# Attention scores: the whole-array block in front of the row pairs, and a later mix

## The chip, the cores and the metric

The kernel runs on one core of a Trainium2 chip. The metric is the device time of one execution in microseconds (us); the median of several runs is compared.

## What is computed

The inputs have batch 4, 12 heads, 448 positions and 64 channels a head. The first part is an attention with a sigmoid in place of the softmax; its result goes through a gated network whose input is mixed with the position before, and this through a network with a Fourier transform ahead of it:

```python
def _attn_ref(q, k, v):
    S = q.shape[2]
    scores = np.matmul(q, k.transpose(0, 1, 3, 2)) / np.sqrt(q.shape[-1]) - np.log(S)
    return np.matmul(1.0 / (1.0 + np.exp(-scores)), v)

def _moe_ref(x, mu_k, mu_r, w_k, w_v, w_r):
    x_prev = ...                      # x, one position earlier
    xk = mu_k * x + (1.0 - mu_k) * x_prev
    xr = mu_r * x + (1.0 - mu_r) * x_prev
    k = np.maximum(xk @ w_k, 0.0)
    v = k * k @ w_v
    return v / (1.0 + np.exp(-(xr @ w_r)))

def _moe2_ref(x, w_ch1, w_ch2):
    u = x + np.real(np.fft.fft(np.fft.fft(x, axis=1), axis=2))
    un = (u - mean(u)) / np.sqrt(var(u) + 1e-06)
    return u + np.maximum(un @ w_ch1, 0.0) @ w_ch2
```

The change lies in the attention and in the first mix (xk).

## The kernel before

Two heads of one batch make a pair; there are 24 pairs, six a batch. For a pair the scores are made transposed, keys on the partitions, in seven blocks of up to 128 x 448 (`places`): three row pairs, in which the two heads use the upper and the lower 64 rows of the TensorE array at the same time (blocks 0 and 1, 2 and 3, 4 and 5), and one block that uses the whole array for the last keys of both heads (`FULL`, block 6). Each block goes to ScalarE (ACT), which takes the sigmoid into a tile `sg` (`weigh`). The blocks of the row pairs are in PSUM banks of a pool of five (`ps2`), in rotation, so the sixth block of a pair takes the bank of its first; the whole-array block is in a pool of three (`ps1`), which the value product and the keys use too.

The first six pairs (`WHOLE`) use 32-bit matmuls. From pair 6 on, q and k are split in a high and a low part, and each block is three matmuls (high by high, low by high, high by low). There `scores` issues the whole-array block first in pairs 6 and 7 and last in pairs 8 to 23.

`attnv` then multiplies the seven sigmoid tiles with v: the value product, tile `av`. `join` copies it to x on ACT, stores x to memory for a later stage, and mixes it with the position before (`mix`: ACT scales, VectorE adds, ACT and VectorE split the result in a high and a low part `xkh` and `xkl`). When a batch has its six mixes, `keys` multiplies them with `w_k`: 8 tiles of 18 matmuls a batch, tile `k`.

The order of every engine's instructions is written by a planner at build time (`Order`). It keeps a clock `now` that TensorE's instructions advance by charged costs; every task is a generator that yields the time at which it goes on. `others()` lets tasks that are due issue their work, but no key matmul. `issued(key)` waits until the planner has noted that key; it adds no instruction and no semaphore. Key matmuls wait in a queue (`feed`) and are issued one by one when nothing else is due. The loop is `attention`: pass i issues the value product of pair i - 1, then the scores of pair i, and then holds the next pass until `PACE` = 10.8 planner microseconds have gone since its start, if there is key work (`pace`). What the planner charges is not what the chip takes.

At the same time `prepare` loads and splits q, k and v of later pairs, and `weights` loads and converts weights on VectorE at a pace of its own (`EVERY`). Behind the attention the rest of the keys runs, and then the other stages, to which nothing is changed.

Of the kernel before, what the change touches and what calls it, by code (L numbers as in the profile page):

```python
# [27 lines left out]
GF = 256  # L28
NG = FF2 // GF
TOK = B * S  # L30
PACE = 10.8
EVERY = (11.6, 9.4)

SL = np.r_[np.arange(2, 129, 2), np.arange(1, 128, 2)]
# [210 lines left out]
def build(tc, ap):  # L245
    nc = tc.nc
    V, G = nc.vector, nc.gpsimd
    o = Order(nc)
# [81 lines left out]
    def bank(name):  # L330
        return ps1.tile([128, 512], F32, tag="bank", name=name)
# [16 lines left out]
    pairs = [(b, p) for b in range(B) for p in range(NP)]  # L348
    WHOLE = NP
# [26 lines left out]
    FULL = len(places) - 1  # L376

    def weigh(i, n, ps):
        sg = att.tile([128, S], F32, tag="sg", name=f"sg_{i}_{n}", bufs=len(places) + 1)
        o.at["sg", i, n] = o.act(sg, ps[:, 0:S], AF.Sigmoid, bias=bias_s, scale=1.0 / math.sqrt(DH))  # L380
        sg_t[i, n] = sg

    def scores(i):
        k, q = pair_t["k", i], pair_t["q", i]

        def rows(j):
            return slice(0, 128) if j is None else slice(64 * j, 64 * j + 64)

        def room(n):
            name = f"sc_{i}_{n}"  # L390
            return bank(name) if n == FULL else ps2.tile([128, 512], F32, tag="sc", name=name)

        if i < WHOLE:
            for n in [FULL, *range(FULL)]:
                c, j = places[n]
                ps = room(n)
                o.mm(ps[:, 0:S], k[rows(j), c], q[rows(j)], True, True, 0.760 if j is None else 0.447)
                weigh(i, n, ps)
                yield from o.others()
        else:  # L400
            halves = [(2 * c, 2 * c + 1) for c in range(3)]
            for ns in [(FULL,), *halves] if i < WHOLE + 2 else [*halves, (FULL,)]:
                ps = {n: room(n) for n in ns}
                for t, (a, b) in enumerate(((0, 0), (0, 1), (1, 0))):
                    for n in ns:
                        c, j = places[n]
                        cost = None if j is None else 0.107
                        o.mm(ps[n][:, 0:S], k[a][rows(j), c], q[b][rows(j)], t == 0, t == 2, cost)
                for n in ns:
                    weigh(i, n, ps[n])  # L410
                yield from o.others()
        o.at["pair", i] = o.now

    def attnv(i, ps):
        v = pair_t["v", i]
        for n in [FULL, *range(FULL)]:
            yield from o.need(("sg", i, n))
            c, j = places[n]
            sg = sg_t.pop((i, n))
            if j is None:  # L420
                o.mm(ps[:, 0:S], v[:, c].rearrange("p j d -> p (j d)"), sg, True, False, 0.760, skip=True)
            else:
                me = slice(64 * j, 64 * j + 64)
                o.mm(ps[me, 0:S], v[:, c, j], sg, False, c == 2, 0.432, skip=True)
            yield from o.others()
        o.at["av", i] = o.now
        o.spawn(join(i, ps), o.now + 0.2)

    def join(i, ps):
        x = att.tile([128, S + 1], F32, tag="x", name=f"x_{i}")  # L430
        G.memset(x[:, 0:1], 0.0)
        yield o.act(x[:, 1 : S + 1], ps[:, 0:S])
        b, p = pairs[i]
        o.dma(x_d[b][p], x)
        if b > 1:
            yield from o.issued(("key", b - 2))
        xh = mop.tile([128, S], F32R, tag=f"xkh{p}", name=f"xkh_{i}")
        xl = mop.tile([128, S], F32R, tag=f"xkl{p}", name=f"xkl_{i}")
        xk_t[b, p] = (xh, xl)
        yield from mix(x, mu_k, att, p, f"k{i}", xh, xl, ("xk", b, p))  # L440
        o.at["mixed", i] = o.now

    def mix(x, mu, pl, p, nm, xh, xl, key, bufs=2):
        xk = pl.tile([128, S], F32, tag="mix", name=f"mix_{nm}", bufs=bufs)
        yield o.act(xk, x[:, 1 : S + 1], AF.Copy, scale=mu[:, 0, p : p + 1])
        yield o.stt(xk, x[:, 0:S], mu[:, 1, p : p + 1], xk, ALU.mult, ALU.add)
        yield o.act(xh, xk)
        o.at[key] = t = o.sub(V, xl, xk, xh)
        yield t
# [6 lines left out]
    def attention():  # L456
        for i in range(len(pairs) + 1):
            t0 = o.now
            if i > 0:
                yield from o.need(("v", i - 1), ("sg", i - 1, FULL))  # L460
                if i > 2:
                    yield from o.issued(("mixed", i - 3))
                yield from attnv(i - 1, bank(f"av_{i - 1}"))
            if i < len(pairs):
                yield from o.need(("k", i), ("q", i))
                yield from scores(i)
            yield t0 + pace()
        yield from o.need(("xk", B - 1, NP - 1))
        o.at["attention"] = o.now

    def pace():
        return PACE if o.feed else 0.0

# [872 lines left out]
```

## Time and profile before

| | us |
|---|---|
| median of 3 runs | 1226.49 |
| lowest, highest | 1226.11, 1231.38 |
| the profiled execution | 1231.31 |
| its span, first to last instruction | 1229.5 |
| granted TensorE clock over the span | 1.000 (the 2.4 GHz level) |

In the trace PE is the matmuls of TensorE, PEld its weight loads, DVE VectorE, ACT ScalarE, POOL GpSimd, SP the engine that issues the DMAs. Rows have times from the span's start; a row of the timeline gives start, duration, engine, line, operation, and what it writes and reads (out<-in). A matmul's duration covers its pipeline, so the rows of matmuls that follow each other overlap; the step from start to start is what one costs. The tiles are named sc (scores), sg (sigmoid), av (value product), x (its copy), mix_k (the mix) and k (keys).

### The profile page before, as it was taken

Reading aid. Unit: us, or ns where it says so; the run is one execution under the profiler, and the core shown is the slowest. Engines: PE = TensorE matmul, PEld = TensorE weight load, DVE = VectorE, ACT = ScalarE, POOL = GpSimd, SP = SyncE. Lnnn points to the kernel's source line nnn. Section 1 sums busy time; section 2 is a strip of 40 time slices with the busy share of each in tenths; the row PEclk is TensorE's granted clock in tenths of the full one; section 3 lists DMA queues with packets and bytes.
Section 4 is the critical chain, followed back from the end, with each engine's and each line's share of the span. In section 5 each row is a group of like instructions: output and inputs, shape, how many; then the busy total and the mean of one; then the engine's idle time right before and its main releaser. Section 6 shows DMA issues by size and latency. Waiting matters only on the chain. (4 is left out here: it accounts for less than half of the span.)

```text
span 1229.5 us, 16416 instructions
## 1 busy us (share of the span) xinstructions
PE 1216.5 (99%) x6142; PEld 1050.5 (85%) x6142; DVE 907.4 (74%) x1425; ACT 479.1 (39%) x864; POOL 135.3 (11%) x97
## 2 busy tenths in 40 slices
PE   8999999999999999999989999999999999999998
PEld 3467766789999998999979999999999999999998
DVE  5776887656853669797999999897566776776654
ACT  5867767766530122142333333332132332322220
POOL 0000000000000000000232232222021111121110
PEclk9999999999999999999999999999999999999999
DMA  6656669666948446396555555555842112121102
GB/s 219 223 169 229 213 239 339 237 243 231 320 158 259 169 165 218 113 316 227 184 202 212 184 200 203 201 186 188 314 141 78 52 54 75 52 66 63 52 1 90
DMA packets 77296, 217.82 MB, mean 177 GB/s; under 512 B 9312, under 2 KB 31776, under 8 KB 76576
## 3 DMA queue, kind: packets, MB, share of 16 engines
q1 hardware_dynamic: 76544, 214.37, 50.3%
q0 software_dynamic: 672, 2.40, 0.6%
q8 instruction: 48, 0.79, 0.3%
q14 instruction: 32, 0.26, 0.1%
HBM read 143.84 MB, written 72.90 MB: 176 GB/s over the span
## 5 line engine op out<-in xcount | busy, mean ns | idle before, releaser
L215 DVE TENSOR_TENSOR acc<-acc,f 128x448 f32<-128x448 f32 x258 | 156.6, 616 | 66.4 <-PE f L180 63.8
L180 PE MATMUL f<-h,w2h 128*128 128x448 f32 x576 | 165.6, 368 | 3.6 <-DVE acc L215 3.6
L180 PE MATMUL f<-un,w1h 128*128 128x448 f32 x576 | 166.2, 368 | 0.0
L180 PE MATMUL f<-h,v2h 128*128 128x448 f32 x576 | 163.6, 365 | 0.0
L180 PEld LDWEIGHTS f<-h,w2h 128*128 128x128 f32 x576 | 107.8, 188 | 14.9 <-DVE acc L215 4.8
L234 ACT ACTIVATE sg<-sc,bias_s 128x448 f32<-128x448 f32 x168 | 95.0, 651 | 60.7 <-PE sc L180 60.7
L180 PEld LDWEIGHTS f<-un,w1h 128*128 128x128 f32 x576 | 108.2, 188 | 10.4 <-issue 0.4
L180 PEld LDWEIGHTS f<-h,v2h 128*128 128x128 f32 x576 | 108.2, 188 | 8.5
L180 PE MATMUL v<-k,wvh 128*128 128x448 f32 x384 | 113.4, 370 | 0.8 <-DMA k<-k_d 0.7
L180 PE MATMUL f<-un,w1l 128*128 128x448 f32 x288 | 105.9, 368 | 0.0
L180 PE MATMUL f<-h,w2l 128*128 128x448 f32 x288 | 105.9, 368 | 0.0
L180 PE MATMUL f<-h,v2l 128*128 128x448 f32 x288 | 105.2, 365 | 0.0
L223 DVE SCALAR_TENSOR_TENSOR w_bits<-w_raw,w_bits 128x768 uint32<-128x768 uint32 x80 | 99.9, 1248 | 1.0
L180 PE MATMUL av<-sg,v 128*64 128x448 f32 (+1 forms) x336 | 81.1, 549 | 0.0
L180 PEld LDWEIGHTS v<-k,wvh 128*128 128x128 f32 x384 | 71.6, 188 | 8.1 <-DMA k<-k_d 2.4
L215 POOL TENSOR_TENSOR v2l<-v,v2h 128x768 fp32r<-128x768 f32 x24 | 46.8, 1970 | 275.0 <-ACT v2h L232 275.0
L215 POOL TENSOR_TENSOR w1l<-w,w1h 128x768 fp32r<-128x768 f32 x20 | 41.2, 2062 | 300.6 <-ACT w1h L232 295.5
L180 PE MATMUL v<-k,wvl 128*128 128x448 f32 x192 | 70.8, 369 | 0.0
L180 PE MATMUL k<-xkh,wkh 128*128 128x448 f32 x192 | 70.7, 368 | 0.0
L180 PE MATMUL k<-xkl,wkh 128*128 128x448 f32 x192 | 70.4, 367 | 0.0
L180 PE MATMUL k<-xkh,wkl 128*128 128x448 f32 x192 | 70.3, 366 | 0.0
L180 PEld LDWEIGHTS av<-sg,v 128*64 128x64 f32 (+1 forms) x336 | 27.9, 144 | 42.5 <-issue 35.9
(175 smaller groups left out, 2356.7 us busy)
## 6 DMA issues: line engine op xcount, KB each, us to landing
w_raw<-in_w SPq DMA_DIRECT2D x40, 768.0 KB, 4.5
w_d<-w SPq DMA_DIRECT2D x40, 384.0 KB, 2.6
k_d<-kp SPq DMA_DIRECT2D x32, 448.0 KB, 2.8
k<-k_d SPq DMA_DIRECT2D x32, 448.0 KB, 6.3
a<-w_d SPq DMA_DIRECT2D x24, 384.0 KB, 3.5
v<-w_d SPq DMA_DIRECT2D x24, 384.0 KB, 3.0
k<-in_k SPq DMA_DIRECT2D x24, 256.0 KB, 5.5
v<-in_v SPq DMA_DIRECT2D x24, 256.0 KB, 3.0
```

Source lines behind the costliest of these rows:

```text
L180: self.nc.tensor.matmul(out, lhs, rhs, start=start, stop=stop, skip_group_check=skip)
L215: eng.tensor_tensor(out, a, c, op=op)
L223: self.nc.vector.scalar_tensor_tensor(out, a, scalar, c, op0=op0, op1=op1)
L234: self.nc.scalar.activation(out, a, fn, **kw)
```

## The change

`PACE` falls from 10.8 to 10.6. From pair 8 on the whole-array block is issued first too. In `join`, behind the copy and the store of x, the mix of pair i is held back until the planner has issued the scores of pair i + 1; the last pair's mix is not held.

```diff
--- before.py
+++ after.py
@@ -28,7 +28,7 @@
 GF = 256
 NG = FF2 // GF
 TOK = B * S
-PACE = 10.8
+PACE = 10.6
 EVERY = (11.6, 9.4)
 
 SL = np.r_[np.arange(2, 129, 2), np.arange(1, 128, 2)]
@@ -399,7 +399,7 @@
                 yield from o.others()
         else:
             halves = [(2 * c, 2 * c + 1) for c in range(3)]
-            for ns in [(FULL,), *halves] if i < WHOLE + 2 else [*halves, (FULL,)]:
+            for ns in [(FULL,), *halves]:
                 ps = {n: room(n) for n in ns}
                 for t, (a, b) in enumerate(((0, 0), (0, 1), (1, 0))):
                     for n in ns:
@@ -432,6 +432,8 @@
         yield o.act(x[:, 1 : S + 1], ps[:, 0:S])
         b, p = pairs[i]
         o.dma(x_d[b][p], x)
+        if i + 1 < len(pairs):
+            yield from o.issued(("pair", i + 1))
         if b > 1:
             yield from o.issued(("key", b - 2))
         xh = mop.tile([128, S], F32R, tag=f"xkh{p}", name=f"xkh_{i}")
```

## Rows read from the trace of the kernel before

**Rows 1.** The page: busy time, share of the span and instructions of each engine.

```profile
PE 1216.5 (99%) x6142; PEld 1050.5 (85%) x6142; DVE 907.4 (74%) x1425; ACT 479.1 (39%) x864; POOL 135.3 (11%) x97
```

**Rows 2.** Waits of PE's matmuls: engine, line, releaser; us in total, times, longest.

```profile
PE f L180 <- DVE acc L215: 3.6, 2, 2.0
```

**Rows 3.** Windows, one pass (pair 8): us; busy us (instructions) by engine; clock, DMA.

```profile
66.56:78.09 11.53, 11.53 (x63) 8.05 (x61) 8.56 (x14) 9.17 (x18) 0.10 (x1) 1.00 0.59 187
```

**Rows 4.** Waits of the weight loads (PEld) from 62 to 250 us: total, times, longest.

```profile
PEld sc L180 <- ACT sg L234: 4.6, 16, 0.3
```

**Rows 5.** Timeline, pair 10, row pairs first: start us, us, engine, line, operation, out<-in.

```profile
89.64 0.48 PE L180 MATMUL sc<-qh,kh 64*128 64x448 f32 x2
...
90.55 1.16 ACT L234 ACTIVATE sg<-sc,bias_s 128x448 f32<-128x448 f32 x2 [2.29 <-PE sc L180]
...
91.60 0.53 ACT L232 COPY x<-av 128x448 f32<-128x448 f32 x1
92.01 2.75 ACT L234 ACTIVATE sg<-sc,bias_s 128x448 f32<-128x448 f32 x5
...
92.04 0.47 PE L180 MATMUL sc<-qh,kh 128*128 128x448 f32 x1
...
92.75 0.36 PE L180 MATMUL k<-xkl,wkh 128*128 128x448 f32 x1
...
92.96 0.36 PE L180 MATMUL k<-xkh,wkl 128*128 128x448 f32 x1
...
94.60 0.72 ACT L234 ACTIVATE mix_k<-x,mu_k 128x448 f32<-128x448 f32 x1
...
97.82 3.32 PE L180 MATMUL av<-sg,v 128*128 128x448 f32 x14
```

**Rows 6.** Timeline, pair 6, whole-array block first; the last row is pass 7's value product.

```profile
49.11 0.47 PE L180 MATMUL sc<-qh,kh 128*128 128x448 f32 x1
...
49.63 0.36 PE L180 MATMUL sc<-qh,kl 128*128 128x448 f32 x1
...
49.92 0.47 PE L180 MATMUL sc<-qh,kh 64*128 64x448 f32 x2
...
50.02 0.64 ACT L234 ACTIVATE sg<-sc,bias_s 128x448 f32<-128x448 f32 x1 [1.41 <-PE sc L180]
...
50.56 0.53 ACT L232 COPY x<-av 128x448 f32<-128x448 f32 x1
...
50.97 2.22 ACT L234 ACTIVATE sg<-sc,bias_s 128x448 f32<-128x448 f32 x4
...
52.48 3.85 PE L180 MATMUL av<-sg,v 128*128 128x448 f32 x14
```

**Rows 7.** Timeline, pair 7, whole-array block first, and the first key matmuls behind it.

```profile
56.26 0.47 PE L180 MATMUL sc<-qh,kh 128*128 128x448 f32 x1
...
56.41 0.54 ACT L232 COPY x<-av 128x448 f32<-128x448 f32 x1 [0.18 <-issue]
...
57.73 0.66 ACT L234 ACTIVATE mix_k<-x,mu_k 128x448 f32<-128x448 f32 x1
...
58.29 1.15 ACT L234 ACTIVATE sg<-sc,bias_s 128x448 f32<-128x448 f32 x2
...
59.76 0.47 PE L180 MATMUL k<-xkh,wkh 128*128 128x448 f32 x1
...
60.07 0.36 PE L180 MATMUL k<-xkl,wkh 128*128 128x448 f32 x1
```

**Rows 8.** Timeline, the value products of passes 4 and 6.

```profile
31.00 3.42 PE L180 MATMUL av<-sg,v 128*128 128x448 f32 x14
...
45.52 3.66 PE L180 MATMUL av<-sg,v 128*128 128x448 f32 x14
```

**Rows 9.** Timeline, pass 23: the value product and the first scores.

```profile
234.95 3.32 PE L180 MATMUL av<-sg,v 128*128 128x448 f32 x14
...
243.56 0.47 PE L180 MATMUL sc<-qh,kh 64*128 64x448 f32 x2
```

## The prediction

> **What bounds the kernel now.** I read the page first, then who TensorE waits for, then one pass of the attention loop row by row. TensorE is busy for 99% of the span, the other engines for much less [rows 1], and over the whole program the waits of its matmuls are small: two waits on VectorE far behind the stage of the change come to 3.6 us [rows 2]. In the stage of the change one pass of the loop takes 11.53 us, of which PE is busy 11.53 us, DVE 8.56 and ACT 9.17 [rows 3]; this row is typical of the passes of pairs 8 to 21. So the stage ends when TensorE's program is through: keys, scores and values share one in-order queue, there is always key work in it, and a stall of TensorE is paid in full. What does not delay TensorE here is free.
>
> "Busy 100%" does not mean that there is no stall, since a matmul row covers its pipeline too. The weight-load rows show it: in the sixteen passes with split scores behind pair 7, a score weight load stood idle for a sigmoid 16 times, 4.6 us in all, 0.3 us at most [rows 4]. Therefore I count from start to start, not busy time.
>
> **The old pass (pair 10) [rows 5].** Scores start at 89.64, the whole-array block at 92.04, the first key matmul at 92.75: 3.11 us. The first sigmoid starts 0.91 us after the first score matmul. The sixth row block needs the bank of the first (five banks), so it waits for that sigmoid; from the start of the sigmoid of block 0 to the end of the third row pair it is 92.04 - 90.55 = 1.49 us. The key matmuls then run from 92.75 to 97.82, 25 of them at 0.20 us; from the first to the second it is 0.21 us.
>
> **Whole-array block first.** Pairs 6 and 7 already run in the new order, so the trace before holds the experiment. In pair 6 [rows 6] ACT takes the sigmoid of the whole-array block at +0.91 us (50.02 - 49.11), then the copy of the previous pair's product (50.56), and the sigmoid of block 0 only at +1.86 (50.97). The row pairs end 1.51 us behind its start, at 52.48: scores take 3.37 us. In pair 7 [rows 7] the sigmoid of block 0 starts at 58.29 and the end comes at 59.76, 1.47 us later; scores take 3.50 us, because a mix stood on ACT in front of block 0's sigmoid (57.73 to 58.29). So three passes say: the scores end 1.5 us after block 0's sigmoid starts. Putting two ACT steps (about 0.95 us) in front of that sigmoid, and only 0.8 us of matmuls (49.11 to 49.92), makes the wait for the bank longer, not shorter.
>
> Will pairs 8 to 21 look like pair 6? The copy is spawned 0.2 us of planner time behind the value product; the planner charges the three whole-array matmuls 0.61 us before it lets others issue. So the copy falls behind the whole-array sigmoid and in front of block 0's, as in pair 6. In the old order the same rule put it behind the sigmoids of blocks 0 and 1 [rows 5]. So: 3.37 - 3.11 = +0.26 us. The first key matmul after row pairs takes 0.31 us to the second instead of 0.21 (59.76 to 60.07) [rows 7]: +0.10. Sum **+0.36 us a pair**. Bounds: pair 7's 3.50 us gives +0.49; a copy that goes ahead of the whole-array sigmoid gives block 0's sigmoid at 0.91 + 0.53 = 1.44, an end at 2.94, and -0.07 a pair. I take pair 6, whose ACT order is the one worked out. 14 pairs x 0.36 = **+5.0 us**.
>
> Part of the +0.36 is the turn between array shapes: from the whole-array matmuls to the first row pair it is 0.29 us (49.63 to 49.92) [rows 6], where matmuls of one shape follow at 0.20. The Trainium skill, "TensorEngine Tiling (Array Packing)", section "Tiling Modes" (Key Properties), says that a change of tiling mode drains the engine, which speaks against one more change a pair. If a drain were a whole matmul of 0.36 us, an estimate from the row durations, the sum by that rule would be some 14 x 0.26 = 3.6 us higher; the row shows a turn 0.09 us longer, and it decides.
>
> Pairs 22 and 23: their operands come late in the plan, and in pass 23 the scores start 8.61 us behind the value product (234.95 to 243.56) [rows 9], with key matmuls between. There the copy is issued ahead of the scores, which is the case with -0.07: -0.1 us for both.
>
> **Mix held back.** In pairs 8 to 21 the mix already stands behind all seven sigmoids (94.60, the last ones from 92.01) [rows 5]. With the whole-array block first, its copy would be ready earlier in the plan and the mix would slip in between the sigmoids; the hold keeps it where it is. Nobody waits for it there: it adds a polling wait to the planner's task alone, no semaphore; the copy and the store of x (SP's queue) are issued before the hold, POOL's memset too, and keys of a batch start only after its last mix. Cost 0; if that cover were gone, the keys of a batch would start later, but up to 24 key matmuls of the batch before (4.9 us) lie in front.
>
> It changes the start. In passes 5 to 7 no key work lies between scores and value product, and a mix stands among the sigmoids. The value product took 3.66 and 3.85 us in passes 6 and 7, 3.42 us in an undisturbed one [rows 6, 8]: -0.24 and -0.43 us. In pair 7 the mix in front of block 0's sigmoid goes (0.56 us) [rows 7], and with the copy ahead of everything (56.41) that wait goes with it: up to -0.56. Bounds 0 and -1.2 us; I take **-1.2 us**, since the hold puts the mix behind all seven sigmoids in each.
>
> **PACE 10.8 to 10.6.** It lets 0.2 us less key work into a pass: 24 matmuls instead of 25. No matmul is added or removed; the left ones run behind the last pair, where keys end the stage anyway. The value product comes 24 x 0.20 = 4.9 us after the scores; its last sigmoid is done about 5.2 us after the scores' start, 3 us before it. Cost 0. It could only act on waits between engines, and there is none in these passes but the one above.
>
> **Sum.** +5.0 - 0.1 - 1.2 = +3.7 us. The profiled execution took 1231.31 us (span 1229.5); with the change 1235.0 (span 1233.2). It lies 4.8 us above the median of 1226.49, so on the median: **1230.2 us**, +0.3%. I count as a difference what exceeds 0.5%, 6.1 us, about what a measurement can tell here; the forecast is "no change, on the slow side".
>
> **Rivals.**
> (a) *Copy first*: if the planner issues the copy ahead of the scores in all late pairs, as in pass 7 (56.41) [rows 7], the wait for the bank vanishes: 16 x -0.07 - 1.2 = -2.3, **1224.2 us**. For it: passes 7, 22, 23 do so. Against: it needs operands that are late in the plan, and in pairs 8 to 21 the scores follow the value product at once.
> (b) *Another ACT step in front of block 0's sigmoid*, slower: one cast of k or q, or a key tile's activation, that comes due there adds about 0.56 us to the wait, as the mix did in pair 7. With five such pairs of 14 the sum passes +6.1 us; with half of them it is 3.7 + 3.9, **1234.1 us**; with all, 1238. For it: the shorter pass shifts where key tiles end. Against: in the old passes nothing but the copy fell so early, all 16 waits being at most 0.3 us [rows 4], and the value product (3.3 us) gives key tiles time to be evacuated before scores begin.
> (c) *The change does nothing to TensorE*: the wait is hidden, sum near 0, **1226.5 us**. Against: TensorE's queue is in order, and pair 6 shows it unhidden.
> (d) *The waits behind the stage move*: the two waits of 3.6 us [rows 2] may vanish or as much may come, on top of the forecast: **1226.6 or 1233.8 us**.
>
> **How the numbers follow.** Forecast 0.60, (a) 0.15, (b) 0.13, (c) 0.05, (d) 0.07. Slower by over 0.5% (above 1232.6): 0.11 of (b), 0.03 of (d), and 0.04 of the forecast, where pair 7's +0.49 a pair applies (14 x 0.49 = 6.9 us): 0.18. Faster by over 0.5% (below 1220.4) only where (a) or (d) also saves waits further on: 0.06. Within: 0.76. The range runs from a little below (a) to (b) with half the pairs, 1223.5 to 1234.2; about 0.16 is left out.
>
> **What would show it.** Scores of pairs 8 to 21 at 3.37 us, block 0's sigmoid at +1.86 behind whole-array sigmoid and copy; the weight loads' wait for sigmoids up from 4.6 to about 7 us; 24 key matmuls a pass, the first step 0.31; value products 6 and 7 near 3.42. It is wrong if the copy stands ahead of the whole-array sigmoid (then a), if scores exceed 3.5 us in many pairs (b), or if the stages behind the attention change length by microseconds (d).

## The result and the profile after

The changed kernel takes 1234.66 us (median of 7 runs, 1231.98 to 1239.72) against 1226.49. The ratio is 1.0062 with an interval of 1.0036 to 1.0088: **7.6 us slower** (4.4 to 10.8). The forecast was +3.7 us. The median lies 0.5 us above the upper end of the range, 1234.2; the ratio on the old median gives 1234.1, just inside it. The forecast called anything within 0.5% "no change" and gave 0.18 to a slowdown above that: 0.62% is above it, but the interval holds 0.5% as well.

The page: TensorE is as full as before; its busy time is 5.1 us higher for the same 6142 matmuls.

```profile
PE 1221.6 (99%) x6142; PEld 1048.4 (85%) x6142; DVE 908.4 (73%) x1425; ACT 481.1 (39%) x864; POOL 134.5 (11%) x97
```

The span grew by 7.9 us (1229.5 to 1237.4). This is where it grew, by the starts of the first matmul of each kind in the two timelines (the 4.2 us behind the start of the last matmul are the same in both):

| stretch | before, us | after, us | difference |
|---|---|---|---|
| start of the span to the first score | 4.65 | 4.92 | +0.27 |
| first score to first value product | 5.29 | 6.25 | +0.96 |
| first value product to first key matmul (pairs 1 to 7) | 49.82 | 50.13 | +0.31 |
| first key matmul to the end of the keys (pairs 8 to 23) | 223.28 | 229.24 | **+5.96** |
| the stages behind (receptance, values, networks) | 942.3 | 942.7 | +0.4 |

The loss lies in the passes with split scores. What scores "take" is counted from the start of their first matmul to the start of the first matmul behind them. Pair 10, the timeline (start us, us, engine, line, operation, out<-in):

```profile
90.22 0.47 PE L180 MATMUL sc<-qh,kh 128*128 128x448 f32 x1
...
91.13 0.64 ACT L234 ACTIVATE sg<-sc,bias_s 128x448 f32<-128x448 f32 x1 [1.96 <-PE sc L180]
...
91.66 0.53 ACT L232 COPY x<-av 128x448 f32<-128x448 f32 x1
...
92.08 3.27 ACT L234 ACTIVATE sg<-sc,bias_s 128x448 f32<-128x448 f32 x6
...
93.59 0.47 PE L180 MATMUL k<-xkh,wkl 128*128 128x448 f32 x1
...
93.90 0.37 PE L180 MATMUL k<-xkh,wkh 128*128 128x448 f32 x1
...
95.69 0.73 ACT L234 ACTIVATE mix_k<-x,mu_k 128x448 f32<-128x448 f32 x1
```

Against [rows 5] the whole-array block comes first. ACT takes its sigmoid at +0.91 us, then the copy (91.66), then block 0's sigmoid at +1.86 (92.08 - 90.22). The first key matmul starts at 93.59: the scores take 3.37 us instead of 3.11, and the first key step is 0.31 instead of 0.21. The mix (95.69) stands behind all sigmoids. This is pair 6 of [rows 6] again.

The waits of the weight loads from 62 to 260 us (us in total, times, longest), against [rows 4]:

```profile
PEld sc L180 <- ACT sg L234: 7.3, 16, 0.9
PEld k L180 <- issue: 6.4, 18, 0.7
```

Again 16 waits for a sigmoid, now 7.3 us instead of 4.6; and 18 short pauses before a key weight load, the turn from row pairs to the whole array.

Two places were not as forecast. Pair 7, whose scores took 3.50 us before [rows 7]:

```profile
53.47 3.76 PE L180 MATMUL av<-sg,v 128*128 128x448 f32 x14
...
56.51 0.72 ACT L234 ACTIVATE mix_k<-x,mu_k 128x448 f32<-128x448 f32 x1
...
57.16 0.47 PE L180 MATMUL sc<-qh,kh 128*128 128x448 f32 x1
...
57.68 0.68 DVE L223 SCALAR_TENSOR_TENSOR mix_k<-x,mu_k,mix_k 128x448 f32<-128x448 f32 x1
...
57.82 0.47 PE L180 MATMUL sc<-ql,kh 128*128 128x448 f32 x1 [0.19 <-DVE ql L215]
...
58.40 0.57 ACT L232 CAST xkh<-mix_k 128x448 fp32r<-128x448 f32 x1 [1.17 <-DVE mix_k L223]
...
58.87 0.63 ACT L234 ACTIVATE sg<-sc,bias_s 128x448 f32<-128x448 f32 x1
...
61.30 0.47 PE L180 MATMUL k<-xkh,wkh 128*128 128x448 f32 x1
```

Pair 7's scores take 4.14 us (57.16 to 61.30). The held mix comes to ACT at 56.51; its VectorE half starts at 57.68; ACT's next instruction, the cast that splits the mix, waits for it until 58.40; the whole-array sigmoid stands behind that cast and starts at 58.87, +1.71 instead of +0.91. Part of it is TensorE's own: its second matmul waits for the low part of q (57.82, 0.35 us late), which VectorE also gives later than before. The value product at 53.47 still took 3.76 us.

And pair 20, where a cast of q comes between the whole-array sigmoid and the copy:

```profile
206.92 0.47 PE L180 MATMUL sc<-qh,kh 128*128 128x448 f32 x1
...
207.83 0.64 ACT L234 ACTIVATE sg<-sc,bias_s 128x448 f32<-128x448 f32 x1 [3.64 <-PE sc L180]
...
208.36 0.56 ACT L232 CAST qh<-q 128x448 fp32r<-128x448 f32 x1
...
208.82 0.54 ACT L232 COPY x<-av 128x448 f32<-128x448 f32 x1
...
209.24 3.27 ACT L234 ACTIVATE sg<-sc,bias_s 128x448 f32<-128x448 f32 x6
...
210.76 0.47 PE L180 MATMUL k<-xkh,wkl 128*128 128x448 f32 x1
```

Block 0's sigmoid starts at +2.32 us (209.24 - 206.92), the scores take 3.84 us.

### The profile page after: what moved, and what is told of

Its sections match the earlier page's. It is cut to its first block, busy times and chain, and to the rows that moved or that the text cites. A ratio compares the mean times of both kernels' runs of the same rounds, so it can differ in the third digit from the quotient of the medians.

```text
span 1237.4 us, 16417 instructions
## 1 busy us (share of the span) xinstructions
PE 1221.6 (99%) x6142; PEld 1048.4 (85%) x6142; DVE 908.4 (73%) x1425; ACT 481.1 (39%) x864; POOL 134.5 (11%) x97
## 4 chain that ended last, share of the span: by engine, by line
PE 84%; issue 10%; POOL 2%; ACT 2%; DMA 1%; DVE 0%; SPq 0%; POOLq 0%; DVEq 0%
PE f L180 33%; PE k L180 10%; PE v L180 9%; PE r L180 7%; PE av L180 6%; PE sc L180 4%; PE f_X L180 4%; PE f_Z L180 4%; PE f_W L180 4%; PE f_Y L180 2%; DMA k<-k_d 1%; POOL w1l L215 1%; PE pq L180 1%; POOL w2l L215 1%; ACT sg L234 1%
```

## The experiments

Every ratio is to the kernel before on the same chip.

**e1: the order alone**

```diff
-            for ns in [(FULL,), *halves] if i < WHOLE + 2 else [*halves, (FULL,)]:
+            for ns in [(FULL,), *halves]:
```

> Only the order of the blocks is changed: whole-array block first in all split pairs; PACE 10.8, no hold. If the longer wait for the sixth block's bank and the extra turn are the cause, the scores of pairs 8 to 21 take 3.37 us against 3.12, the first key matmul behind them 0.31 against 0.21, and the time lies 5 to 6 us above the kernel before. If the new pace or the hold carry the loss, it is within 2 us of before.

Measured: 1232.21 us, ratio 1.0052 (1.0032 to 1.0071), +6.4 us. From the first key matmul to the end of the keys it takes 229.25 us, as with the whole change (229.24). Pair 10:

```profile
91.18 0.47 PE L180 MATMUL sc<-qh,kh 128*128 128x448 f32 x1
...
93.04 2.22 ACT L234 ACTIVATE sg<-sc,bias_s 128x448 f32<-128x448 f32 x4
...
94.53 0.47 PE L180 MATMUL k<-xkl,wkh 128*128 128x448 f32 x1
...
95.12 0.70 ACT L234 ACTIVATE mix_k<-x,mu_k 128x448 f32<-128x448 f32 x1
...
95.68 1.19 ACT L234 ACTIVATE sg<-sc,bias_s 128x448 f32<-128x448 f32 x2
```

Scores take 3.35 us (91.18 to 94.53). Without the hold the mix (95.12) slips in between the sigmoids, and nothing is lost by it: the last two sigmoids start at 95.68, while the value product follows some 5 us behind the scores. So the order carries nearly the whole loss, and in these passes the hold buys nothing.

**e2: the hold alone**

```diff
+        if i + 1 < len(pairs):
+            yield from o.issued(("pair", i + 1))
```

> Only the mix is held back; row pairs first as before, PACE 10.8. My prediction took -1.2 us for it (value products of passes 6 and 7 and the scores of pair 7 without their waits). The trace of the changed kernel speaks against that: there the scores of pair 7 take 4.14 us instead of 3.50, because the split of the held mix (cast of xkh) stands on ACT in front of the whole-array sigmoid. By that reading the early passes together are 0.3 us longer, and the time is within 1 us of before.

Measured: 1227.74 us, ratio 1.0007 (0.9993 to 1.0021). The early stretch is 50.14 us against 49.82; pair 7's scores take 4.15 us, the value products of passes 6 and 7 3.35 and 3.70 us. The hold alone brings back the whole early shape of the changed kernel: what it gives to the value products (0.24 and 0.08 us), pair 7 loses twice over (0.65 us).

**e3: the pace alone**

```diff
-PACE = 10.8
+PACE = 10.6
```

> Only PACE is 10.6. If a shorter pass only moves key matmuls behind the last pair, the time is within 1 us of before, the scores stay at 3.12 us and 24 key matmuls stand in a pass. If the pace makes operands late or brings ACT work in front of the sigmoids, scores grow in some pairs and the time rises by 2 us or more.

Measured: 1227.38 us, ratio 1.0006 (0.9992 to 1.0020). All sixteen scores take 3.10 to 3.13 us; the stretch to the end of the keys is 222.48 us against 223.28. There are 24 key matmuls in a pass, as forecast. The pace costs nothing that can be told.

**e4: the kernel before, two banks exchanged**

```diff
-            return bank(name) if n == FULL else ps2.tile([128, 512], F32, tag="sc", name=name)
+            own = n == FULL if i < WHOLE else n == FULL - 1
+            return bank(name) if own else ps2.tile([128, 512], F32, tag="sc", name=name)
```

> The kernel before, with its order, hold-free and PACE 10.8; only the PSUM banks are exchanged: in split pairs the sixth row block takes its bank from the pool of three and the whole-array block takes the sixth place in the pool of five. The order of TensorE's and ACT's instructions is that of before. If the wait of the sixth block for block 0's sigmoid is a real stall of TensorE, the third row pair falls from 1.08 to 0.70 us, the scores of 16 pairs from 3.12 to 2.74, and the time by 6 us. If that wait is hidden, nothing moves.

Measured: 1220.58 us, ratio 0.9956 (0.9941 to 0.9971), 5.4 us **faster** than before. Pair 10:

```profile
88.99 0.47 PE L180 MATMUL sc<-qh,kh 64*128 64x448 f32 x2
...
89.91 1.16 ACT L234 ACTIVATE sg<-sc,bias_s 128x448 f32<-128x448 f32 x2 [1.59 <-PE sc L180]
...
90.32 0.36 PE L180 MATMUL sc<-qh,kh 64*128 64x448 f32 x2
...
91.02 0.47 PE L180 MATMUL sc<-qh,kh 128*128 128x448 f32 x1
...
91.73 0.37 PE L180 MATMUL k<-xkl,wkh 128*128 128x448 f32 x1
...
91.94 0.37 PE L180 MATMUL k<-xkh,wkl 128*128 128x448 f32 x1
```

The third row pair lasts from 90.32 to 91.02, 0.70 us as reckoned, the scores 2.74 us (88.99 to 91.73), in the sixteen pairs 2.74 to 2.76; no weight load of a score waits for a sigmoid any more. The stall was real, though the page shows TensorE at 99%. This is the fastest of all versions tried.

**e5: the changed kernel, the same exchange**

The edit of e4 on the changed kernel.

> The changed kernel with the same exchange of banks: sixth row block from the pool of three, whole-array block in the pool of five. The wait of the sixth block goes, the extra turn between array shapes stays. Expected: scores of split pairs 3.37 to 2.95 us (third row pair 1.24 to 0.82 or less), first key step still 0.31, 16 x 0.43 = 6.9 us below the changed kernel, that is about the time of the kernel before (+1 us) and some 6 us above the kernel before with the exchange. If the turn were the larger part of the loss, it would stay 4 us or more above the kernel before.

Measured: 1224.61 us, ratio 0.9983 (0.9966 to 0.9999): about 10 us below the changed kernel, and 3.3 us above e4 where some 6 were expected. Pair 10:

```profile
87.86 0.47 PE L180 MATMUL sc<-qh,kh 128*128 128x448 f32 x1
...
90.01 0.36 PE L180 MATMUL sc<-qh,kh 64*128 64x448 f32 x2
...
90.71 0.47 PE L180 MATMUL k<-xkh,wkl 128*128 128x448 f32 x1
...
91.02 0.36 PE L180 MATMUL k<-xkh,wkh 128*128 128x448 f32 x1
```

Scores take 2.85 us (87.86 to 90.71), less than the 2.95 expected: once the wait is gone, the third row pair needs 0.70 us like that of e4. The rest against e4 is the turn: 2.85 - 2.74 = 0.11 us in the scores and 0.31 - 0.21 = 0.10 at the first key matmul (90.71 to 91.02). From the first key matmul to the end of the keys it is 220.06 us against e4's 218.02. So with no wait in either, the order costs 2.0 us in the trace (3.3 us by the ratios). The trace shows too little of it: over pairs 8 to 23 the scores take 1.6 us more in sum (45.4 against 43.8 us), and 13 more first key steps are long, 1.4 us; but e4's other key matmuls happened to run at a mean step of 0.2054 us and e5's at 0.2038 (the last section has these two steps), which hides 0.9 us.

So with no wait the order costs 0.11 + 0.10 = 0.21 us a pair, 3.0 us in all; with the wait it costs 0.25 + 0.10 = 0.35. The wait takes 3.12 - 2.74 = 0.38 us a pair in the old order and 3.37 - 2.85 = 0.52 in the new one, 0.14 more, and the waits of the weight loads rise by 7.3 - 4.6 = 2.7 us in all, less than half of the 5.96. The two parts don't simply add: as long as the sixth block waits, the scores end some 1.5 us behind the sigmoid, so the 0.11 us of turn ahead of it lies in time that the wait takes anyway. Neither part makes the loss alone. The expectation compared e5 with the kernel before, and this can't tell them apart, since the exchange also takes away the 0.38 us that the kernel before was already paying; e5 against e4 can.

**e6: the changed kernel, the copy first**

```diff
-        o.spawn(join(i, ps), o.now + 0.2)
+        if i < WHOLE + 1:
+            o.spawn(join(i, ps), o.now + 0.2)
+        else:
+            o.spawn(join(i, ps), o.now)
+            yield from o.others()
```

> The changed kernel, but the copy of the value product to x is issued ahead of the scores from pair 7 on (the planner's task is started at once). My rival (a): block 0's sigmoid starts at 1.44 us instead of 1.86, scores take 2.95 us instead of 3.37, and the time falls by some 6 us below the changed kernel, to within 2 us of before. If it is the whole-array sigmoid alone that delays block 0's, the time stays where the changed kernel is.

Measured: 1229.65 us, ratio 1.0021 (1.0008 to 1.0034): about 5 us below the changed kernel, but still 2.6 us above before. Pair 10:

```profile
89.87 0.47 PE L180 MATMUL sc<-qh,kh 128*128 128x448 f32 x1
...
90.04 0.54 ACT L232 COPY x<-av 128x448 f32<-128x448 f32 x1 [1.22 <-PE av L180]
...
90.78 0.64 ACT L234 ACTIVATE sg<-sc,bias_s 128x448 f32<-128x448 f32 x1 [0.20 <-PE sc L180]
...
91.60 3.26 ACT L234 ACTIVATE sg<-sc,bias_s 128x448 f32<-128x448 f32 x6 [0.18 <-PE sc L180]
...
93.11 0.47 PE L180 MATMUL k<-xkh,wkl 128*128 128x448 f32 x1
```

The copy is out of the way (90.04), but block 0's sigmoid starts at +1.73 us, not +1.44: now it waits for its own scores, which come behind the whole-array block. The scores take 3.24 us; in the sixteen pairs 3.19 to 3.24. So the copy was a part of the delay, and the matmuls of the whole-array block in front of the first row pair are a floor under it.

**e7: the changed kernel, the first mixes not held**

```diff
-        if i + 1 < len(pairs):
+        if WHOLE < i < len(pairs) - 1:
             yield from o.issued(("pair", i + 1))
```

> The changed kernel, but the mixes of pairs 0 to 6 are not held back. A look at passes 5 to 7 alone: if the held mix puts the cast of xkh in front of the whole-array sigmoid of pair 7, that pair's scores fall from 4.14 us to 3.50 as before, and the value product of pass 6 rises again from 3.35 to 3.59; from the first value product to the first key matmul 49.8 us instead of 50.1. The rest as in the changed kernel.

In one execution the early stretch is 49.82 us, pair 7's scores 3.50, the value product of pass 6 3.60 us. So the held mix made pair 7's 4.14 us. The one time, 1234.36 us, tells nothing at this size.

**e8: the kernel before, two sigmoids exchanged**

```diff
-                for n in ns:
+                for n in (ns[::-1] if 0 in ns and i > WHOLE + 1 else ns):
                     weigh(i, n, ps[n])
```

> The kernel before, but in pairs 8 to 23 ACT takes the sigmoid of block 1 ahead of that of block 0; order of TensorE, banks, PACE and mix as before. It makes the wait for block 0's bank longer by one sigmoid (0.53 us) and changes nothing else. If the scores end 1.5 us behind the start of block 0's sigmoid, they take 3.65 us instead of 3.12 and the time rises by 16 x 0.53 = 8.5 us. If TensorE's order (the turns) is what costs, nothing moves.

Measured: 1226.44 us, ratio 0.9997 (0.9982 to 1.0011). Nothing moved; the scores took 3.12 us:

```profile
89.40 0.47 PE L180 MATMUL sc<-qh,kh 64*128 64x448 f32 x2
...
91.81 0.47 PE L180 MATMUL sc<-qh,kh 128*128 128x448 f32 x1
...
92.52 0.37 PE L180 MATMUL k<-xkl,wkh 128*128 128x448 f32 x1
```

This miss corrected my picture. The program of e8 gives the sixth block of pair 10 the bank of block 1, not of block 0: the pool hands out the bank whose reader was issued first. In the kernel before this is block 0's, so the prediction had the right bank, but "five banks in rotation" was the wrong reason. The sixth block waits for whichever row-pair sigmoid ACT takes first, and e8 had not changed when that one starts.

**e9: the kernel before, that sigmoid twice**

```diff
+        if n == 0 and i > WHOLE + 1:
+            nc.scalar.activation(sg, ps[:, 0:S], AF.Sigmoid, bias=bias_s, scale=1.0 / math.sqrt(DH))
         o.at["sg", i, n] = o.act(sg, ps[:, 0:S], AF.Sigmoid, bias=bias_s, scale=1.0 / math.sqrt(DH))
```

> The kernel before, but in pairs 8 to 23 ACT takes the sigmoid of block 0 twice, into the same tile; the result is the same, TensorE's order as before. The exchange of two sigmoids moved nothing, because the sixth block was given the bank of the block whose sigmoid stands first. Here the bank that is free first is block 0's behind the second sigmoid, 0.53 us later. If the bank wait is paid by TensorE one for one, the scores take 3.65 us instead of 3.12 and the time rises by 16 x 0.53 = 8.5 us. ACT has 0.53 us a pass more, of 11.5; if ACT or nothing were the bound, less than 2 us come.

Measured: 1237.32 us, ratio 1.0080 (1.0056 to 1.0103), +9.8 us. Pair 10:

```profile
91.34 0.47 PE L180 MATMUL sc<-qh,kh 64*128 64x448 f32 x2
...
92.25 0.63 ACT L381 ACTIVATE sg<-sc,bias_s 128x448 f32<-128x448 f32 x1 [1.25 <-PE sc L180]
...
92.92 1.17 ACT L234 ACTIVATE sg<-sc,bias_s 128x448 f32<-128x448 f32 x2
...
94.39 0.47 PE L180 MATMUL sc<-qh,kh 128*128 128x448 f32 x1
...
95.11 0.36 PE L180 MATMUL k<-xkl,wkh 128*128 128x448 f32 x1
```

The second sigmoid starts 0.67 us behind the first, not 0.53. The whole-array block starts at 94.39, 1.47 us behind it; the scores take 3.77 us, 0.66 more than before, and 16 x 0.66 = 10.6 us. TensorE's order and array turns are those of before, so the wait for the bank costs by itself, nearly one for one (+9.8 of 10.6 us).

## Why the prediction was half the size

- **The bound, right.** TensorE's queue through the split passes is what counts; e4 (-5.4 us, 16 x 0.38 = 6.1 taken away) and e9 (+9.8 us, 10.6 added) move the time by nearly what they take from or add to one wait. The prediction did not name the largest wait of a matmul in the program, 4.7 us for the first load of q; it lies at the start of the span.
- **+0.36 us a pair, right in size, and its parts too.** Pairs 8 to 21 take 3.35 to 3.37 us but for pair 20. The rule that the scores end 1.5 us behind a sigmoid's start holds in e1 (94.53 - 93.04 = 1.49), e6 (93.11 - 91.60 = 1.51) and e9 (94.39 - 92.92 = 1.47). What failed is the word "block 0" in it (e8): it is the row-pair sigmoid that ACT takes first, in e9 its second run. With no wait the turn is 0.11 us in the scores and 0.10 at the key matmul, by e5 against e4; the prediction's rows had 0.09 and 0.10. The Trainium skill ("TensorEngine Tiling (Array Packing)", section "Tiling Modes") says that a change of tiling mode drains the engine, and gives no price. My estimate of a whole matmul for it would have been 0.26 us more a pair, and these rows do not have it.
- **Fourteen such pairs, too few.** The term of pairs 22 and 23 (-0.1 us) failed: in the changed kernel pair 22 takes the full 3.37 us, its operands being there in time, and only pair 23 starts late (3.11 us). Pair 20 was an instance of rival (b), +0.47 us from one cast. Together the passes lost 5.96 us in the trace where I had 4.9: 4.2 in the scores (54.1 against 49.9 us in sum), 1.4 in 13 more long first key steps, and 0.3 because the other key matmuls happened to run at a longer mean step (0.2046 against 0.2040 us; last section).
- **The hold, wrong in sign.** I took -1.2 us, the good end of the bounds, from undisturbed value products alone. I followed the mix's first step on ACT and left out its next: a cast that waits for VectorE, in the same in-order queue, in front of pair 7's first sigmoid; the low part of pair 7's q comes later as well. e2 and e7 show the whole of it: +0.3 us with the hold, nothing without. This is 1.5 us of the shortfall.
- **The pace, right:** e3 shows 24 key matmuls a pass and no difference in time.
- **Rival (a), mis-sized.** I reckoned 0.91 + 0.53 from ACT's side alone; the row pair's scores are not there before +1.7 us. Copy first does not break even (e6).
- **What stays open.** 5.96 + 0.3 = 6.3 us is what the trace of the attention accounts for. The remaining 1.6 us of the 7.9 in the trace are 1.2 before the first value product, where the eleven programs profiled here are alike and still range from 9.92 to 11.18 us, and 0.4 in the stages behind. Whether any of it is the change's can't be told; the measured interval, 4.4 to 10.8 us, holds 6.3 as well, and the fastest executions of the two kernels, 1231.98 and 1225.38 us, are 6.6 us apart. The single parts give 6.4 + 0.9 + 0.7 = 8.0 us, and only the first of them is clear of zero.

## What to carry to other kernels

When a tile needs a buffer that an earlier tile of the same group must free, look at what stands in front of that evacuation, on its engine's queue and among the matmuls that feed it: in every run here that had the wait, the stalled row pair ended 1.47 to 1.52 us behind the evacuation's start (pairs 8 to 23), so all that delayed the start was paid. Count the turns between array shapes too: here the new order cost 0.21 us a pair even where nothing waited. Look for a stall in the steps from start to start and in the weight loads' waits, since a busy share of 99% hides it, and before reordering the work, ask whether another free buffer removes the wait altogether: here exchanging two banks was worth 5.4 us with not one instruction moved. Follow a task that is held back through all of its steps on every in-order queue that it will meet later, not its first step alone.

## What the runs showed of the hardware that was not expected

The same chain of matmuls, each with its own weight load, ran at one of two steps for a long time. The chain of the kernel before (start us, us, what):

```profile
641.48 254.62 PE f L180 x1230
...
929.14 14.59 PE f L180 x72
```

and of e4:

```profile
635.39 250.59 PE f L180 x1230
```

The same 1230 matmuls take 254.62 us (0.2070 us each) in the one and 250.59 us (0.2037) in the other, with the granted clock at the 2.4 GHz level in both; later in the kernel before, 72 matmuls take 14.59 us (0.2026). In the timelines the step of the slower stretches is 0.206 to 0.207 us throughout and that of the faster ones alternates around 0.203; most of the changes lie where the engine was interrupted, but in the changed kernel the step rose at 710 us in the middle of a chain, with no step over 0.207 us there. The key matmuls of the attention have the same two steps: in pair 10 they follow at 0.203 us in the kernel before and at 0.207 in e4, so stretches of the trace that differ by a microsecond or less can differ by this alone. From the first matmul of the second network to the last this gives 702.1 to 702.7 us in six of the profiles (before, after, e2, e3, e8, e9), and 697.8 to 699.5 in the other five. The profiled executions of the first kind lay 2.8 to 4.8 us above the median of their kernel, those of the other kind with more than one run (e1, e4, e5, e6) between 0.5 below and 1.4 above. Most of the spread between executions of one kernel is probably this; what sets the step was not tried.
